# Batch 1's q loads placed between the gate/value and the out-projection weights, with new emission orders for every chunk

## Chip, cores, metric

One core of one Trainium2 chip. The metric is the device time of one execution in microseconds; a kernel's figure is the median of its runs. Profile times count from the start of the profiled span, which is about 2 us shorter than the device time.

## The reference, cut to what matters

```python
# 8 batches x 8 heads, 576 positions, head dim 64
q_s = softmax over the last dim of q;  k_s = softmax over the sequence of k
kv  = einsum('bhsd,bhse->bhde', k_s, v)
att = einsum('bhsd,bhde->bhse', q_s, kv)          # -> x: 4608 tokens x 512
out = (silu(x @ w_gate) * (x @ w_val)) @ w_out    # 512 -> 1536 -> 512
```

The attention is small. The feed-forward block is nearly all of TensorE's work and consumes `x` in chunks of 512 tokens.

## The kernel before

Engines run programs fixed at build time. The author writes the order as strings of tokens ("plans"), one plan for each kind of chunk; each token emits instructions on one or more engines, and each engine executes its own instructions in the order of emission. The tokens:

- `a`..`g`, `v`, `G`, `U`, `I`, `J`: first feed-forward product. `A`..`F`, `H`, `O`, `S`: out-projection; `E` and `H` also emit four stores each.
- `eq`, `ek`, `ns`, `cv`: exponentials, row sums and v cast of a coming batch. `nm0`, `nm1`: GpSimd product that normalizes q, and the DMA transpose of its result, for head groups 0 and 1.
- `load`: six loads (q, k, v for two head groups) of the batch after that. `kv`: the k-v matmuls. `xx`: the attention output, the first reader of the transposed q.

```python
def load(b, G, what, src, after=None):
    raw[what, b, G] = ld.tile([128, 2, T * 64], FP32, tag=what, ..., bufs=2 if what == "v" else 3)
    d = nc.sync.dma_start(out=raw[what, b, G], in_=ap)
    if after is not None:
        tc.add_manual_dep(d.ins, after.ins.name, SYNC, reason="order of loads")
...
def tr_dma(b, G):
    qt = at.tile([128, T, 2, 64], BF16, tag="qtd", name="qtd")
    nc.sync.dma_start_transpose(out=qt..., in_=s["qs"]...)      # same queue as the loads
...
elif nm == "nm":
    norm_mul(b, G, nc.vector if alt else nc.gpsimd)
    tr_dma(b, G)
elif nm == "lo":
    ...
    load_group(b + 1, 0)
    load_group(b + 1, 1)
elif nm == "xx":
    x_pair(b, nc.scalar if alt else nc.vector)   # matmuls xa, xz: first half reads
                                                 # transpose 0, second half transpose 1
...
PLAN = """
S002 G4 S022 S102 a0 b0 G10 d0 c0 A v0 a1 S042 eq0 S122 S142 S302 B S342 f0 S242
b1 ek0 U4 S322 D S222 ek1 e0 eq1 cv0 S202 C* v1 cv1 g0 ns0 F E d1 H* a2 ns1 c1 f1
silu nm0 b2 c2 nm1 e1 g1 d2* v2 a3 U10 f2 e2 load kv b3 g2 c3 d3 G5 v3 e3* f3 xx*
X0 G11 U5 X1 U11 g3* X3 X2
"""
```

`PLAN_B` is the prologue, `PLAN_0` chunk 0, `PLAN` the steady chunks 1 to 5, `PLAN_N` and `PLAN_E` the rest.

The softmax here doesn't subtract the row's maximum and nothing guards it: scores larger than these inputs give would overflow.

## Time and profile before

| | before |
|---|---|
| median time | 303.1 us (3 runs, 302.94 to 306.04) |
| TensorE busy / idle | 289.9 / 10.9 us of 300.8 |
| TensorE waits over 0.5 us | 2.6, 1.1, 1.0, 0.7 us, all before 76 us |
| steady chunk, start to start | 30.3 us |

TensorE's idle time is the quantity to watch: where it works without pause, only its instruction count and its clock set the time, and the change leaves the count as it is. The clock is given as the share of full speed that was granted: 1.00 is full, 0.50 is half. The prediction shows the lines.

### The profile page before, as it was taken

The page shows a single profiled execution, that of the slowest core. Times are in us where ns is not written, and L with a number is a line of the kernel's source. Part 1 is how long each engine was busy: PE and PEld are TensorE (multiplying, and loading weights), DVE is VectorE, ACT ScalarE, POOL GpSimd, SP SyncE. Part 2 cuts the span into 40 slices and gives each one's busy share as a digit, 9 for nine tenths or more (in the row PEclk, how much of TensorE's full clock was granted, in tenths as well). Part 3 has the DMA queues.
Part 4 walks back from the last instruction along what each step waited for, and adds up shares of the span by engine and source line. Part 5 has one row for each costly group of instructions (what it writes and reads, how often), then busy time and mean ns, then how long its engine had stood idle before and what let it go on. Part 6 is the DMA issues. An engine that isn't in the chain of part 4 may idle for free.

```text
span 300.8 us, 6895 instructions
## 1 busy us (share of the span) xinstructions
PE 289.9 (96%) x2644; PEld 227.9 (76%) x2644; DVE 232.3 (77%) x497; ACT 210.8 (70%) x385; POOL 136.6 (45%) x108
## 2 busy tenths in 40 slices
PE   8999978999999999999999999999999999999993
PEld 6878744577688758875887588758886888888882
DVE  3943846778898887888788778878888898895981
ACT  5754367787698579957994899489948776667530
POOL 1840156468208900890089008910794465275500
PEclk9999997999999999999999999999999999999999
DMA  7999999999002992289229931992190000600066
GB/s 268 265 173 207 224 396 316 313 252 327 0 3 60 161 391 83 55 174 375 92 49 175 352 117 29 200 360 105 39 183 0 2 0 4 139 3 0 2 140 140
DMA packets 38863, 46.43 MB, mean 154 GB/s; under 512 B 16304, under 2 KB 21936, under 8 KB 38832
## 3 DMA queue, kind: packets, MB, share of 16 engines
q1 hardware_dynamic: 33024, 41.30, 47.9%
q0 software_dynamic: 5808, 4.72, 10.2%
q8 instruction: 20, 0.33, 0.4%
q14 instruction: 11, 0.09, 0.1%
HBM read 37.75 MB, written 9.44 MB: 157 GB/s over the span
## 4 chain that ended last, share of the span: by engine, by line
PE 79%; DMA 14%; POOL 2%; DVE 1%; ACT 1%; SPq 0%; issue 0%; ACTq 0%; POOLq 0%; DVEq 0%
PE sx L384 20%; PE ox L526 14%; PE sw L384 10%; PE ow L526 7%; PE g_ps L435 7%; PE u_ps L435 7%; DMA wo<-in_moe_w_out_dram 6%; PE sy L384 5%; PE oy L526 3%; DMA qtd<-qs 3%; PE o_ps L473 3%; PE kv L192 3%; DMA v<-in_v_dram 3%; DMA q<-in_q_dram 2%; POOL wg L104 1%; POOL wv L104 1%
## 5 line engine op out<-in xcount | busy, mean ns | idle before, releaser
L418 POOL TENSOR_TENSOR hr<-sg,s 128x512 bf16<-128x512 f32 (+1 forms) x29 | 37.9, 1307 | 75.9 <-DVE s L417 74.9
L384 PEld LDWEIGHTS <-gt 128*128 128x128 f16 x576 | 56.2, 98 | 10.5 <-issue 0.7
L426 POOL TENSOR_TENSOR hr<-sg,s 128x512 bf16<-128x512 f32 (+1 forms) x28 | 35.6, 1271 | 35.4 <-ACT sg L425 35.4
L384 PE MATMUL sx<-xs,gt 128*128 128x256 f16 (+1 forms) x288 | 42.7, 271 | 0.0
L116 ACT COPY s<-sx 128x512 f32<-128x512 f32 (+1 forms) x66 | 38.2, 579 | 5.0 <-PE sx L384 4.2
L526 PEld LDWEIGHTS <-hs 128*128 128x128 bf16 x384 | 37.6, 98 | 5.4
L417 DVE TENSOR_TENSOR s<-sw,s 128x512 f32<-128x512 f32 (+1 forms) x36 | 24.5, 682 | 17.7 <-PE sw L384 17.4
L425 ACT ACTIVATE sg<-sx 128x512 f32<-128x512 f32 (+1 forms) x36 | 21.2, 590 | 19.9 <-PE sx L384 14.7
L152 POOL TENSOR_TENSOR qs<-eq,rr 128x1152 bf16<-128x1152 bf16 x14 | 29.5, 2120 | 10.5 <-DVE rr L147 10.5
L384 PEld LDWEIGHTS <-wg 128*128 128x128 f16 x288 | 27.7, 98 | 5.2
L421 DVE TENSOR_TENSOR s<-sx,s 128x512 f32<-128x512 f32 (+1 forms) x36 | 24.5, 680 | 8.9 <-ACT s L116 4.7
L526 PEld LDWEIGHTS <-hr 128*128 128x128 bf16 x288 | 28.2, 98 | 3.3
L410 ACT ACTIVATE sg<-s 128x512 f32<-128x512 f32 (+1 forms) x36 | 22.5, 626 | 8.0 <-DVE s L408 7.9
L143 DVE TENSOR_REDUCE rs<-eq 128x18 f32<-128x1152 bf16 x16 | 21.5, 1343 | 8.5 <-ACT eq L127 8.5
L116 ACT COPY s<-sw 128x512 f32<-128x512 f32 (+1 forms) x34 | 19.8, 583 | 8.9 <-PE sw L384 3.8
L408 DVE TENSOR_TENSOR s<-sy,s 128x512 f32<-128x512 f32 (+1 forms) x36 | 24.3, 675 | 1.6 <-ACT s L116 1.1
L435 PE MATMUL g_ps<-xt,wg 128*128 128x512 f16 (+1 forms) x96 | 24.3, 375 | 0.0
L526 PE MATMUL ox<-wt,hs 128*128 128x256 f16 x192 | 23.6, 273 | 0.0
L435 PE MATMUL u_ps<-xt,wv 128*128 128x512 f16 (+1 forms) x96 | 23.4, 375 | 0.0
L384 PE MATMUL sy<-xt,wg 128*128 128x256 f16 (+1 forms) x144 | 21.4, 271 | 0.0
L384 PE MATMUL sx<-xt,gt 128*128 128x256 f16 (+1 forms) x144 | 21.4, 271 | 0.0
L384 PE MATMUL sw<-xs,wv 128*128 128x256 f16 (+1 forms) x144 | 21.4, 271 | 0.0
(99 smaller groups left out, 571.4 us busy)
## 6 DMA issues: line engine op xcount, KB each, us to landing
q<-in_q_dram SPq DMA_DIRECT2D x16, 576.0 KB, 6.0
k<-in_k_dram SPq DMA_DIRECT2D x16, 576.0 KB, 8.3
v<-in_v_dram SPq DMA_DIRECT2D x16, 576.0 KB, 8.4
out_dram<-o_sb SPq DMA_DIRECT2D x72, 128.0 KB, 2.4
wo<-in_moe_w_out_dram POOLq DMA_DIRECT2D x3, 512.0 KB, 18.3
wg<-in_moe_w_gate_dram POOLq DMA_DIRECT2D x2, 512.0 KB, 11.5
wv<-in_moe_w_val_dram POOLq DMA_DIRECT2D x2, 512.0 KB, 13.0
wg<-in_moe_w_gate_dram POOLq DMA_DIRECT2D x2, 256.0 KB, 5.5
```

Of the source, the lines that this page charges most:

```text
L116: nc.scalar.copy(out=out, in_=in_)
L143: nc.vector.reduce_sum(out=rs, in_=s["eq"].rearrange("p t h d -> p (t h) d"), axis=mybir.AxisListType.X)
L152: eng.tensor_mul(s["qs"].rearrange("p t (h d) -> p (t h) d", d=64), s["eq"].rearrange("p t h d -> p (t h) d"), s["rr"].to_broadcast([128, ...
L384: nc.tensor.matmul(out=bank[:, h * j:h * j + h], lhsT=wgt(kk, j), rhs=rhs[:, kk, 0:h], start=first and j == 0 and kk == 0, stop=kk == 1, s ...
L408: nc.vector.tensor_add(self.s1, self.y[:, 0:w], self.s1)
L410: nc.scalar.activation(out=self.sa[:, 0:w], in_=self.s1, func=AF.Silu)
L417: nc.vector.tensor_add(self.s2, self.w[:, 0:w], self.s2)
L418: meng.tensor_mul(self.out(0), self.halves(self.sa), self.halves(self.s2))
L421: nc.vector.tensor_add(self.s5, self.x[:, 0:w], self.s5)
L426: meng.tensor_mul(self.out(1), self.halves(sb), self.halves(self.s5))
L435: nc.tensor.matmul(out=ps[:, 0:self.n], lhsT=w[:, kk, 128 * self.m:128 * self.m + 128], rhs=xt[:, kk, self.r:self.r + self.n], start=(kk = ...
L526: nc.tensor.matmul(out=dst[p][:, 0:HN], lhsT=lhs(kk, p), rhs=rhs(kk), start=start and i == 0, stop=i == HM - 1, skip_group_check=True,)
```

## The change

The intent: batch 1's q loads wait on the last gate slice rather than on the first out-projection slice, so its exponentials can start earlier; the plans are then reordered to use that. The diff, all five plans cut:

```diff
         tc.add_manual_dep(w_dma[0].ins, dmas["v", 0, 0].ins.name, SYNC, reason="order of loads")
+        load(1, 0, "q", q, after=w_dma[-2])
+        load(1, 1, "q", q)
         for m0 in (0, 4, 8):
             w_dma.append(wo_slice(m0, 4))
+        tc.add_manual_dep(w_dma[-3].ins, w_dma[-4].ins.name, SYNC, reason="order of loads")
...
-        load(1, 0, "q", q, after=w_dma[-3])
-        load(1, 1, "q", q)
         for G in range(NG):
-            load(1, G, "k", k)
+            load(1, G, "k", k, after=w_dma[-3] if G == 0 else None)
             load(1, G, "v", v)
...
         PLAN_B = """   (all of it reordered; its end:)
-        ... O21 xz00 kk1:1 xz01* ns0:2 O22 nm0:2 ek0:2 xz10* O31 cv1:2 xz11 eq1:2 O32 ek1:2
+        ... Q2 xz10 cv0:2 eq1:2 O31 ns0:2 O32 ek1:2 cv1:2 nm0:2
         PLAN_0 = """
-        a0 b0 ns1 load v0 ... c1 Y3 nm1 W0 g0 ... xx* e3 ...
+        a0 b0 G4 Y0 Y2 Y1 c0 ns1 ... d1 load e0 nm1 c1 ... e3 W2 xx* f3 ...
         PLAN = """
-        ... silu nm0 b2 c2 nm1 e1 g1 d2* v2 a3 U10 f2 e2 load kv b3 ... f3 xx* ...
+        ... E ns1 nm0 ek1 b2 g1 load nm1 d2 c2 v2 H* f2 e2 kv silu a3 b3 ... f3 xx* ...
         (PLAN_N and PLAN_E: the same tokens in other orders)
```

More of the change, by code (lines that the diff above doesn't have):

```diff
@@ L744 @@
         PLAN_B = """
-        I0 J0 I1 I2 J1 J2 I3 J3 I4 I5 J4 J5 I6 I7 J6 I8 Q0* J7 J8 I9 I10 Q2* Q1* J9 eq0:1
-        Q3 J10 eq1:1 I11 ns0:1 ns1:1 J11 ek0:1 ek1:1 nd1:1 O01 nd0:1* cv0:1 O11 O02* tr00
-        cv1:1 O12 tr10 tr11 kk0:1 eq0:2 cv0:2 load:2 tr01 O21 xz00 kk1:1 xz01* ns0:2 O22
-        nm0:2 ek0:2 xz10* O31 cv1:2 xz11 eq1:2 O32 ek1:2
+        I0 I1 J0 I2 J1 J2 I3 J3 I4 I5 J4 I6 J5 J6 I7 I8 J7 J8 eq0:1 ns0:1 eq1:1 I9 ns1:1
+        Q0 I10 J9 I11 J10 J11 Q1* O01 O11 ek0:1 O02 Q3* nd0:1* nd1:1* cv0:1 tr00 tr10
+        cv1:1 O21 tr11 ek1:1 tr01 kk0:1 O12 xz00 load:2 kk1:1 xz01* eq0:2 O22 ek0:2 xz11
+        Q2 xz10 cv0:2 eq1:2 O31 ns0:2 O32 ek1:2 cv1:2 nm0:2
 """
         PLAN_0 = """
-        a0 b0 ns1 load v0 Y0 G4 a1 Y2 Y1* kv U4 c0 d0 G10 f0 b1 c1 Y3 nm1 W0 g0 d1 v1 a2
-        e0 f1 e1 b2 c2 g1 d2 W1 v2 U10 a3 f2 G5 b3 g2 v3 e2 c3 d3* xx* e3 U5 f3 W2 X0 X2
-        X1 G11 U11 g3* X3 W3
+        a0 b0 G4 Y0 Y2 Y1 c0 ns1 G10 d0* v0 a1 U4 f0 Y3 W0 G5 b1 g0 d1 load e0 nm1 c1 v1
+        a2 f1 kv g1 b2 d2 e1 c2 v2 a3 f2 b3 c3 e2 U10 g2 d3 v3 e3 W2 xx* f3 U5 X0 W1 G11
+        X1 X3* W3 U11 g3 X2
 """
         PLAN = """
-        S002 G4 S022 S102 a0 b0 G10 d0 c0 A v0 a1 S042 eq0 S122 S142 S302 B S342 f0 S242
-        b1 ek0 U4 S322 D S222 ek1 e0 eq1 cv0 S202 C* v1 cv1 g0 ns0 F E d1 H* a2 ns1 c1 f1
-        silu nm0 b2 c2 nm1 e1 g1 d2* v2 a3 U10 f2 e2 load kv b3 g2 c3 d3 G5 v3 e3* f3 xx*
-        X0 G11 U5 X1 U11 g3* X3 X2
+        a0 b0 c0 G4 d0 G10 v0 a1* f0 S222 b1 A c1 S202 g0 S002 d1 S042 S242 S022 v1 e0
+        S122 B eq0 U4 S322 S102 S142 a2 e1 C S342 D ns0 cv0 eq1 U10 cv1 S302 F f1 ek0 E
+        ns1 nm0 ek1 b2 g1 load nm1 d2 c2 v2 H* f2 e2 kv silu a3 b3 g2 c3 d3* G5 v3 e3* f3
+        xx* U5 G11 X0 X2 X1 g3* U11 X3
 """
         PLAN_N = """
-        a0 b0 c0 d0 A v0 T0* f0 S002 a1 b1 g0 d1 c1 S022 S102 S222 v1 e0 a2 S202 f1 e1 b2
-        S042 c2 g1 d2 v2 S122 B f2 a3 T1 b3 c3 S242 S142 g2 e2 d3 S322 D v3 a4 f3 T2 C g3
-        T3 d4 b4 e3 c4 v4 f4 S302 F a5 g4 b5 S342 d5 v5 e4 c5* f5 E X0 X1 e5* X3 X2* g5*
+        S022 a0 b0 c0 d0 A v0 S042 T0* f0 T1 S142 S222 a1 b1 S122 c1 g0 e0 d1 v1 B f1 a2
+        b2 c2 g1 d2 S002 T2 S102 v2 a3 e1 e2 f2 D T3 g2 b3 d3 c3 v3 a4 f3 S302 b4 C S322
+        g3 v4 S202 d4* e3 c4 f4 a5 e4 b5 g4 d5 c5 S242 v5 S342 F f5 X0* e5 X2 E X1 g5* X3*
         H*
@@ L767 @@
         PLAN_E = """
-        S202 S042 S022 S002 A S142 S122 S102 B C S322 S302 S342 D S222 S242 E F H*
+        S042 S022 S222 A S002 S142 S102 B C S122 D S322 S202 S242 S302 S342 F E H*
 """
```

## The prediction

> **What bounds the kernel now.** I read the page first (busy times, slices), then TensorE's waits, then the chain that ended last, then the timelines of TensorE and of the load queue. The page says that TensorE (PE) is the bound:
>
> ```profile
> PE 289.9 (96%) x2644; PEld 227.9 (76%) x2644; DVE 232.3 (77%) x497; ACT 210.8 (70%) x385; POOL 136.6 (45%) x108
> ...
> PEclk9999997999999999999999999999999999999999
> DMA  7999999999002992289229931992190000600066
> ```
>
> A busy PE is not a PE at its peak, so I checked the pace: twelve 256-column matmuls of `ox` take 1.31 us in the chain, 109 ns each, and hardly vary anywhere after 76 us. So PE works at one steady pace, and its time falls only if idle time or slow clock goes. Idle is 300.8 - 289.9 = 10.9 us, of which about 5.2 us lie after the last matmul (the final copy and store). TensorE's waits name nearly all the rest:
>
> ```profile
> PE o_ps L473 <- DVE hr L324: 2.6, 1, 2.6
> PE warm_ps L256 <- DVE zero L604: 1.1, 1, 1.1
> PE xa L273 <- DMA qtd<-qs: 1.0, 1, 1.0
> PE kv L192 <- POOL vb L118: 0.7, 1, 0.7
> ```
>
> All are before 76 us. The 2.6 us hole (43.4 to 46.0 us) is also the cause of the 7 in the clock row: in one-microsecond windows the granted clock was 0.54, 0.50, 0.50 and 0.75 from 47 to 51 us, a loss of 1.7 us. Its origin is in the chain of waits, beside the second DMA stretch that matters:
>
> ```profile
> 16.33 16.65 DMA wo<-in_moe_w_out_dram
> 33.00 6.77 DMA q<-in_q_dram
> ...
> 65.96 9.55 DMA qtd<-qs
> ```
>
> Batch 1's q load is held until the first out-projection slice lands at 33.0, and itself lands at 39.8; VectorE then stands in its row sums while PE needs the product queued behind them. The DMA row is full for the first 75 us.
>
> **What the Trainium skill says.** (1) "DMA: Bandwidth & Descriptors", section "Queues, rings and completion order": SP owns one ring per DMA engine, and each engine consumes descriptors in ring order. "DMA Transpose (X-bar)" on the same page adds that the plain transpose is issued from SP or ACT; here it shares SP's queue with the loads. The trace agrees: a `qtd` transpose issued behind two stores, or behind another transpose alone, lands in 3.2 to 5.4 us; the only one that follows six loads took 9.6 us and landed 1.1 us after the last of them (65.00 + 9.4 = 74.4 against 65.96 + 9.55 = 75.5). (2) "TensorE: Matmul & The Clock Gate", Part 1: an idle PE falls to half clock, and needs a busy window of about 3.4 us to return. The trace agrees in size: half clock from 47 to 50.75 us, though here 2.6 us of idleness was enough.
>
> **The change, part by part.**
>
> (a) The early q loads. They now wait for the last gate slice, which lands at 14.86 + 13.6 = 28.5 us, in place of 33.0. The last value slice (30.5 us before) is nearly all that shares the DMA with them, so I expect q at 33 to 34.5 us, not 39.8 and 41.2. Row sums then lie before PE's products, and the 2.6 us hole and its 1.7 us of slow clock should go. The weights pay: the first out-projection slice is issued only after the last value slice has landed, so it lands nearer 36 than 33 us. The out-projection starts at 39.5, so that is close, but should hold within 1 us. Up to the start of chunk 0's matmuls (58.2 us) I expect 4 to 5 us gained.
>
> (b) Chunk 0 gives it back. In both kernels the second transpose of batch 2 stands behind six loads of batch 3. The queue:
>
> ```profile
> 58.48 1.35 SPq L180 DMA_TRANSPOSE qtd<-qs  x1
> 59.93 1.86 SPq L462 DMA_DIRECT2D out_dram<-o_sb  x2
> 61.84 0.58 SPq L89 DMA_DIRECT2D q<-in_q_dram  x1
> ...
> 65.00 0.85 SPq L89 DMA_DIRECT2D v<-in_v_dram  x1
> 65.96 5.14 SPq L180 DMA_TRANSPOSE qtd<-qs  x1
> ```
>
> What lets these loads go is the first transpose, after the GpSimd product `nm0`, which the new order puts behind the cast of batch 2's second v. That v landed at 60.2 (52.83 + 7.4); the DMA is full, so I expect it 2 to 3 us earlier at best, plus 1.1 us of cast and 2.1 us of product: transpose at 60 to 61, loads from 62, second transpose landed at about 75 again. PE would arrive near 70, waits some 5 us in place of 1.0, and loses about 1.7 us of clock. Sum of (a) and (b): -5 + 4.5 + 1.7, about +1 us.
>
> (c) The steady chunks. This is the step that I weigh most. The new chunk plan moves `load` from after both transposes to between `nm0` and `nm1`. The compiled order of the changed kernel's load queue confirms it: four stores of E, transpose, six loads, transpose, four stores of H, in chunks 1 to 4 (chunk 5 has no loads left). Before, it was eight stores, two transposes, six loads:
>
> ```profile
> 124.72 5.30 SPq L462 DMA_DIRECT2D out_dram<-o_sb  x8
> 130.14 3.19 SPq L180 DMA_TRANSPOSE qtd<-qs  x2
> 133.39 0.60 SPq L89 DMA_DIRECT2D q<-in_q_dram  x1
> ...
> 136.20 0.94 SPq L89 DMA_DIRECT2D v<-in_v_dram  x1
> ```
>
> The same chunk on PE: E ends at 124.0, and the `qtd` is used at 136.3 and 136.6:
>
> ```profile
> 122.72 1.47 PE L526 MATMUL ow<-wo,hs 128*128 128x256 f16 x12
> ...
> 136.28 0.33 PE L273 MATMUL xa<-qtd,kn 64*64 64x320 bf16 x4
> ...
> 136.55 0.31 PE L273 MATMUL xa<-qtd,kn 64*64 64x320 bf16 x4
> ```
>
> Now the new chunk, counted from the end of E on PE. Store issue starts 0.7 us later (124.0 to 124.72); four stores at 5.30 / 8 = 0.66 us are 2.6 us; the first transpose's issue is 1.4 us; so the loads start at +4.7. From first load issue to last landing the steady chunks show 12.2 to 13.0 us (133.39 to 136.20 + 9.4; 163.99 to 167.01 + 10.0). Only one transpose is ahead now, not two, so up to a microsecond less: 12.1. The transpose lands 1.1 us behind, as in chunk 0: +17.9. PE in the new order has after E thirteen groups of 0.437 us, H of 1.31, `kv` of 1.15 and one G of 0.86: it is at the `xa` at +9.0. The wait is 17.9 - 9.0 = 8.9 us, in a kernel where nothing after it can make up PE time. After nearly 9 us idle the clock is half for a while; from the 1.7 us seen, and 2.6 us that the 64 first warm-up matmuls take beyond 109 ns each (9.6 - 7.0), I take 2.0. Four chunks times 10.9 is 43.6 us.
>
> (d) The remaining reordering (chunks 5 to 8, matmul groups, sums) keeps PE's instruction count; the order had no waits after 76 us, and I take 0, with perhaps half a microsecond in chunk 5. The tail stays.
>
> Sum: 303.1 + 1 + 43.6 = 347.7; I say 347.
>
> **The rivals.**
>
> Rival 1: the prologue gain is all that happens. The 2.6, 1.0, 0.7 and 1.7 us go, and the steady chunks hide the transposes: 297 to 300 us. For it: these plans look tuned, and the title names the landing times. Against it: the changed queue order is a fact of the build, and chunk 0 has already shown what a transpose behind loads costs. It needs the transpose to pass the loads.
>
> Rival 2: the transpose is only partly held, because transfers overlap in the queue or the loads run faster when nothing else moves. DMA moved 390 to 410 GB/s in the full microseconds of 138 to 144 us, so 3.54 MB need 9 us; with first bytes 1.5 us after issue the transpose lands at +16 and the wait is 7 us, with 1 us of clock: 303 + 4 x 8 = 335.
>
> Rival 3: the out-projection weights land too late, and PE waits at 39.5 us. From 2.4 us a slice (33.0 to 35.4 us for the second) I can see 1 to 3 us once; chunk 0's DMA bound would hide part of it. Worth at most 3 us.
>
> **Range and chances.** The mechanism of (c) rests on one measured case but needs no scheduling luck; only its size is soft: 7.8 to 9.5 us a chunk, 1 to 3 us of clock, times four, and 2 us either way in the prologue. That gives about 338 to 354; I widen the low side for rival 2. Range 330 to 356. Rival 1 keeps a few per cent of chance.
>
> **What would show it.** Right: TensorE's waits list `xa` (or its weight load) on DMA `qtd` five times, four of them of 8 to 10 us; the DMA part shows second transposes landing after about 10 us; the clock row dips after each; no `o_ps` wait of 2.6 us near 43 us; `eq` of batch 1 starts before 36 us. Wrong: steady transposes landing in 3 to 5 us although issued behind loads, or PE reaching the `xa` later than 9 us after E because it waits elsewhere (then the wait moves, and my sum counts it under the wrong name). A `o_ps` wait on `wo` would speak for rival 3.

## The result and the profile after

The changed kernel takes **355.92 us** (median of 4, 355.2 to 357.69) against 303.02 us. A ratio in this document is the mean time of one kernel's fast runs over that of the other's fast runs of the same rounds, so it is not quite the ratio of the medians; here it is 1.174 (95% interval 1.164 to 1.184).

The page of the changed kernel, its first part (busy time of engines) and its second (40 slices of the span):

```profile
PE 299.7 (85%) x2644; PEld 228.8 (65%) x2644; DVE 235.2 (66%) x485; ACT 211.4 (60%) x390; POOL 148.7 (42%) x115
...
PEclk9999999996999589995999769995899999999999
DMA  7999998690009900396006920099004500050055
```

The same 2644 matmuls keep TensorE busy for 9.8 us longer (299.7 - 289.9), and idle time grew from 10.9 to 54.0 us (353.7 - 299.7). The clock row has five dips, and each follows a stretch in which the DMA row is full. TensorE's waits name the cause (who waited, for whom, us in total, times, longest):

```profile
PE xa L273 <- DMA qtd<-qs: 39.9, 5, 8.8
PE o_ps L473 <- DMA wo<-in_moe_w_out_dram: 2.1, 2, 1.9
PE sx L384 <- ACT s L116: 1.4, 1, 1.4
```

One kind of wait, five times, holds 39.9 of the 54.0 us of idleness; it was 1.0 us before. The load queue of the changed kernel in chunk 1 (timeline: start, length of the issue, not of the transfer):

```profile
104.36 2.41 SPq L462 DMA_DIRECT2D out_dram<-o_sb  x4
106.88 1.32 SPq L180 DMA_TRANSPOSE qtd<-qs  x1
108.25 0.58 SPq L89 DMA_DIRECT2D q<-in_q_dram  x1
...
112.36 3.54 SPq L180 DMA_TRANSPOSE qtd<-qs  x1
```

and TensorE in the same chunk (timeline, with the wait and its releaser in brackets):

```profile
102.80 1.48 PE L526 MATMUL ow<-wo,hs 128*128 128x256 f16 x12 [0.21 <-DVE hs L502]
...
113.32 0.33 PE L273 MATMUL xa<-qtd,kn 64*64 64x320 bf16 x4
...
122.55 0.48 PE L273 MATMUL xa<-qtd,kn 64*64 64x320 bf16 x4 [8.79 <-DMA qtd<-qs]
```

The first half of `xa` goes through at 113.3 us; the second waits 8.79 us for the transpose that was issued behind six loads. The last of these, issued at 111.80, landed 9.6 us later, at 121.4; the transpose landed at 112.36 + 10.15 = 122.5. What follows runs at half clock. One-microsecond windows of the changed kernel (busy time of PE, PEld, DVE, ACT, POOL, then the granted clock, DMA share, GB/s):

```profile
123.00:124.00 1.00, 1.00 (x10) 0.28 (x3) 0.00 (x0) 0.92 (x3) 0.00 (x0) 0.50 0.11 39
...
126.00:127.00 1.00, 1.00 (x5) 0.47 (x4) 0.80 (x3) 0.13 (x1) 0.00 (x0) 0.51 0.00 0
127.00:128.00 1.00, 1.00 (x7) 0.58 (x6) 0.00 (x0) 1.00 (x2) 0.00 (x0) 1.00 0.00 0
```

From 122.55 to 127.0 the clock is 0.50, which loses half of 4.4 us, 2.2 us.

Where the 52.9 us of added span lie, from the start of each chunk's first `sy` group on TensorE in both timelines. In the kernel before, chunks 1 to 5 open with one `G4` group of 0.86 us ahead of that mark; the table counts it with its own chunk, so that both columns hold the same work:

| stretch | before | after | added |
|---|---|---|---|
| to chunk 0 | 58.55 | 57.02 | -1.5 |
| chunk 0 | 21.25 | 29.73 | +8.5 |
| chunks 1 to 4 | 30.29, 30.28, 30.28, 30.29 | 41.76, 41.24, 40.79, 41.15 | +43.8 |
| chunk 5 | 30.28 | 31.18 | +0.9 |
| the rest | 69.58 | 70.83 | +1.2 |

### The profile page after: what moved, and what is told of

Its sections match the earlier page's. It is cut to its first block, busy times and chain, and to the rows that moved or that the text cites. A ratio compares the mean times of both kernels' runs of the same rounds, so it can differ in the third digit from the quotient of the medians.

```text
span 353.7 us, 6939 instructions
## 1 busy us (share of the span) xinstructions
PE 299.7 (85%) x2644; PEld 228.8 (65%) x2644; DVE 235.2 (66%) x485; ACT 211.4 (60%) x390; POOL 148.7 (42%) x115
## 3 DMA queue, kind: packets, MB, share of 16 engines
q1 hardware_dynamic: 33024, 41.30, 40.3%
## 4 chain that ended last, share of the span: by engine, by line
PE 64%; DMA 25%; DVE 2%; POOL 2%; ACT 2%; issue 1%; SPq 1%; DVEq 0%; POOLq 0%; ACTq 0%
PE sx L384 16%; DMA qtd<-qs 14%; PE ox L526 11%; PE sw L384 7%; PE u_ps L435 7%; PE ow L526 6%; PE g_ps L435 5%; DMA wv<-in_moe_w_val_dram 4%; PE sy L384 4%; DMA wo<-in_moe_w_out_dram 4%; PE oy L526 3%; PE kv L192 2%; DMA v<-in_v_dram 2%; DVE hs L502 2%; DMA q<-in_q_dram 1%
## 5 line engine op out<-in xcount | busy, mean ns | idle before, releaser
L426 POOL TENSOR_TENSOR hr<-sg,s 128x512 bf16<-128x512 f32 (+1 forms) x29 | 37.1, 1278 | 132.1 <-ACT sg L425 132.0
L418 POOL TENSOR_TENSOR hr<-sg,s 128x512 bf16<-128x512 f32 (+1 forms) x31 | 41.1, 1327 | 13.6 <-DVE s L417 13.6
L116 ACT COPY s<-sx 128x512 f32<-128x512 f32 (+1 forms) x59 | 34.1, 579 | 15.4 <-PE sx L384 15.2
L450 DVE TENSOR_TENSOR hr<-sg,u_ps 128x512 bf16<-128x512 f32 (+1 forms) x24 | 16.2, 674 | 40.8 <-PE u_ps L435 40.2
L273 PE MATMUL xa<-qtd,kn 64*64 64x320 bf16 x48 | 4.6, 381 | 39.9 <-DMA qtd<-qs 39.9
L152 POOL TENSOR_TENSOR qs<-eq,rr 128x1152 bf16<-128x1152 bf16 x15 | 32.7, 2181 | 6.0 <-DVE rr L147 6.0
L116 ACT CAST xt<-xa 128x320 f16<-128x320 f32 (+2 forms) x28 | 9.2, 396 | 38.6 <-PE xa L273 38.6
L273 PEld LDWEIGHTS <-kn 64*64 64x64 bf16 x96 | 2.0, 118 | 42.6 <-DMA qtd<-qs 41.3
L435 PE MATMUL u_ps<-xt,wv 128*128 128x512 f16 (+1 forms) x96 | 29.2, 435 | 0.0
L435 PE MATMUL g_ps<-xt,wg 128*128 128x512 f16 (+1 forms) x96 | 28.3, 424 | 0.0
L447 ACT ACTIVATE sg<-g_ps 128x512 f32<-128x512 f32 (+1 forms) x24 | 14.2, 593 | 15.9 <-PE g_ps L435 15.9
```

Source lines behind the costliest of these rows:

```text
L116: nc.scalar.copy(out=out, in_=in_)
L152: eng.tensor_mul(s["qs"].rearrange("p t (h d) -> p (t h) d", d=64), s["eq"].rearrange("p t h d -> p (t h) d"), s["rr"].to_broadcast([128, ...
L418: meng.tensor_mul(self.out(0), self.halves(self.sa), self.halves(self.s2))
L426: meng.tensor_mul(self.out(1), self.halves(sb), self.halves(self.s5))
L435: nc.tensor.matmul(out=ps[:, 0:self.n], lhsT=w[:, kk, 128 * self.m:128 * self.m + 128], rhs=xt[:, kk, self.r:self.r + self.n], start=(kk = ...
```

## The experiments

The theory to test: a transpose that is in flight together with the loads lands only when the loads are done; TensorE waits for it and then runs at half clock. A ring is, as in the prediction, the list of work that one issuing engine has on one DMA engine. The rivals: the new order of everything else costs the time; or the second GpSimd product is late.

**1. The steady loads behind the second transpose.** One token of the changed kernel moves:

```diff
-        ns1 nm0 ek1 b2 g1 load nm1 d2 c2 v2 H* ...
+        ns1 nm0 ek1 b2 g1 nm1 load d2 c2 v2 H* ...
```

> The changed kernel with one token moved: in the steady chunk plan the six loads come right behind the second transpose's issue, not ahead of it; chunk 0 is left as it is. Theory (the transpose is held by the loads ahead of it in its ring): the four steady xa waits of 8.0 to 8.8 us and the 2.2 us of slow clock after each go, so 355.9 - 4 x 10.8 = about 313 us (309 to 316), steady second transposes land within 4 us of issue, and chunk 0's wait of 6.1 us stays. Rival (the new order of the other instructions costs the time, or the second GpSimd product is late): under 10 us gained, above 345 us.

Measured: 311.73 us, ratio 1.025 (1.020 to 1.031). This run's waits, and the summary of its `qtd` tile:

```profile
PE xa L273 <- DMA qtd<-qs: 6.4, 1, 6.4
```

```profile
DMA to landing us min/median/max: 3.2/3.2/10.5
```

The four steady waits are gone, chunk 0's is left, and the transposes land in 3.2 us, although the loads follow directly in the same queue. One token of the order makes 44 of the 53 us. Both rivals fall: the order of everything else stayed.

**2. The same in chunk 0.** As 1, and `load e0 nm1` in `PLAN_0` becomes `e0 nm1 load`.

> As e1_steady_load_last, and in chunk 0 too the loads are put behind the second transpose. Theory: chunk 0's wait of 6.1 us and its 3.0 us of slow clock go as well, so about 9 us less than e1_steady_load_last: 302 to 305 us, no xa wait over 1 us. If the prologue of the changed kernel were itself worth 4 to 5 us, as the prediction had it, 299 us. Rival: chunk 0 is bound by the DMA as a whole, so the wait moves to another consumer and under 4 us is gained over e1_steady_load_last.

Measured: 304.89 us, ratio 1.005 (1.000 to 1.009), 6.8 us below run 1. The five `xa` waits shrank to one of 0.3 us (the profile is of the slowest of the six executions). A wait of 2.7 us of `sx` for ScalarE took part of the place in chunk 0: ScalarE stands in the exponential of a q that lands late. So with all the transposes free, the early q loads and the new order gain nothing over the kernel before.

**3. The reverse: the kernel before with its steady loads moved forward.**

```diff
-        silu nm0 b2 c2 nm1 e1 g1 d2* v2 a3 U10 f2 e2 load kv b3 ...
+        silu nm0 load b2 c2 nm1 e1 g1 d2* v2 a3 U10 f2 e2 kv b3 ...
```

> The kernel before with one token of its steady plan moved: the six loads go between the first and the second product-and-transpose, nothing else of the change. Theory (transposes in flight with loads land only when these are done, PE waits and then runs at half clock): this alone makes most of the loss. The first transpose is issued at about +19.6 us of the chunk, the second lands some 14.5 us later, and PE needs it at +26 us: waits of about 8 us and 2.2 us of clock in four chunks, 303.9 + 4 x 10 = about 344 us (337 to 350). Rival (it takes the whole new order): under 320 us.

Measured: 347.54 us, ratio 1.148. TensorE's waits in this run:

```profile
PE xa L273 <- DMA qtd<-qs: 37.7, 4, 9.9
```

The position of one token is sufficient, with nothing else of the change in the kernel.

**4. The loads in another ring.** Program order as in the changed kernel; the steady loads are issued by ScalarE.

```diff
-                        load_group(b + 1, 0)
-                        load_group(b + 1, 1)
+                        eng = nc.scalar if ci > 0 else nc.sync
+                        load_group(b + 1, 0, eng)
+                        load_group(b + 1, 1, eng)
...   (load and load_group pass eng on)
```

> The changed kernel with its program order kept, but the steady chunks' six loads are issued from ScalarE's queue, so that they have another ring than the transposes, and the same 3.5 MB move at the same time. Theory (order within one ring): the second transpose shares with the loads but no longer stands behind them; it lands in 3 to 6 us in place of 9 to 10, the steady waits fall from 8.5 to 0 to 3 us, total 313 to 328 us (ScalarE pays some 3 us of issue a chunk). Rival (bandwidth: DMA engines full of loads, so any transfer is late): waits stay at 7 us or more, total above 345 us.

Measured: 349.08 us, ratio 1.150. The expectation missed: leaving the loads' ring did not free the transpose. In chunk 1 the two transposes were issued at 107.86 and 110.41 us and landed after 12.2 and 12.0 us. ScalarE had issued its last loads at 111.31 and 113.30, after both transposes, and they landed first: 113.30 + 6.6 = 119.9 against 120.1 and 122.4. Most of the time that TensorE lost was another wait: ScalarE's own instructions stood still for 6.8 us while it issued the loads, and TensorE waited for its copies (`sx` on ScalarE, 28.6 us in 5 waits, against 7.5 us for `qtd`). So this run says nothing on the time without the ring order, but it says that a transpose need not stand behind loads to be late. The DMA part of a 20 us window of this run, with one load group of six (q10, ScalarE's ring), two transposes and some stores (q1), tells why:

```profile
DMA packets 4641, 5.19 MB, mean 260 GB/s; under 512 B 2592, under 2 KB 2592, under 8 KB 4640
...
q10 hardware_dynamic: 1632, 3.54, 48.9%
q1 hardware_dynamic: 3008, 1.64, 40.9%
```

Each load has 272 packets (1,632 / 6). With the 33,024 that the changed kernel's page counts for 48 loads, 72 stores and 12 transposes, a store comes to 80 and a transpose to 1,184; eight stores and two transposes then make the 3,008 of q1. So one transpose moves its 0.29 MB in 1,184 small packets, and six loads their 3.54 MB in 1,632. The Trainium skill says in "DMA: Bandwidth & Descriptors", section "Queues, rings and completion order", that each DMA engine takes turns between rings packet by packet. The same view for 112 to 114 us shows it:

```profile
q10 hardware_dynamic: 304, 0.65, 83.9%
q1 hardware_dynamic: 294, 0.13, 23.2%
```

From 113 to 119 us the loads' ring moved 155 to 167 packets in each microsecond and the transposes' ring 158 to 171: packet against packet, so the transposes got 0.04 MB of a microsecond's 0.39. When the loads ran out, the transposes' ring moved 915 packets in the next microsecond (119 to 120). In the changed kernel, where all share one ring, it looks different: only 0 to 14 packets under 512 B moved in each microsecond from 110 to 119 us, then 492 and 676 in those from 119 and 121 us. There the second transpose came after the loads in the order of the ring. So the transpose is late in either ring, in two different ways.

**5. Work in place of the wait.** In the changed kernel, dummy matmuls between the two halves of `xa`:

```diff
             s = st.pop((b, G))
+            if G == 1 and 2 <= b < B - 1:
+                warm_up(45 if b == 2 else 65)
```

> The changed kernel with added work: between the two halves of the xa matmuls, where PE waits, 45 (chunk 0) or 65 (chunks 1 to 4) dummy matmuls of 256 columns, 4.9 and 7.1 us at full clock, a little shorter than the waits of 6.1 and 8.0 to 8.8 us. Theory (PE's idle time makes its clock fall to half, and this costs 3.0 us in chunk 0 and 2.2 us in each steady chunk beyond the wait): with more work the kernel gets faster by up to 3.0 + 4 x 2.2 = 12 us, 343 to 348 us, and the granted clock after the waits is 1.00. Rival (the slow stretch after the wait is not caused by the idleness): the same 356 us or more, clock still 0.5 after the waits.

Measured: 349.65 us, ratio 1.152: with 305 more matmuls the kernel is some 6 us faster than without them, but not the 8 to 13 us expected. The timeline of TensorE in chunk 1, then windows of the same chunk:

```profile
109.83 7.27 PE L256 MATMUL warm_ps<-zero 128*128 128x256 bf16 x65
119.48 0.33 PE L275 MATMUL xa<-qtd,kn 64*64 64x320 bf16 x4 [2.38 <-DMA qtd<-qs]
```

```profile
119.00:120.00 1.00, 0.52 (x9) 0.26 (x10) 0.00 (x0) 0.14 (x1) 0.00 (x0) 1.00 1.07 408
...
121.00:122.00 1.00, 1.00 (x3) 0.30 (x2) 1.00 (x3) 0.59 (x2) 0.00 (x0) 0.50 0.00 0
```

The dummies ended 2.4 to 2.5 us early in chunks 1 and 2, and the clock fell to 0.50 again. In chunk 0 only 1.0 us of idleness was left, the clock stayed at 1.00, and the chunk takes 26.4 us in place of 29.7. In the third and fourth steady chunks 1.2 and 1.5 us were left, the clock stayed at 1.00, and the periods are 39.3 and 39.5 us in place of 40.8 and 41.2. In chunks 1 and 2, where the clock fell all the same, the periods are no shorter (42.1 us each, against 41.8 and 41.2). So the half clock goes only where the idleness that is left is short, and with it goes its cost; it is the idleness that causes it.

**6. The q loads alone.** The kernel before with the three load edits of the diff, all plans as before.

> The kernel before with only the first part of the change: batch 1's q loads after the last gate slice, the out-projection slices after the last value slice, k after the first of these; all plans as before. Prediction's step (a): the 2.6 us o_ps wait on VectorE and its 1.7 us of slow clock go, 299 to 301 us. Reading of the changed kernel's trace: the out-projection slices land later (last at 44 to 45 us against 39.5 us), PE waits for them 1.7 to 2.1 us in place of the 2.6 us, and chunk 0 is bound by loads anyway: 302 to 304 us, the same within 0.5%.

Measured: 303.23 us, ratio 0.9997 (0.995 to 1.005). The 2.6 us `o_ps` wait on VectorE and the slow clock after it are gone from its profile, as the prediction's step (a) says. But 1.7 us of `o_ps` on the out-projection weights came in, 1.4 us of transposes on `qs`, and `kv` waits for a v cast rose to 3.1 us. The last is not the edit's alone: run 3, whose prologue is that of the kernel before, has a `kv` wait of 2.9 us in its trace. There the hole of 2.1 us cost no clock, and TensorE came to chunk 0 at 56.0 us, not 58.6. That `kv` starts at 61.6 us before, 61.2 in run 3 and 62.2 in run 6, however early chunk 0 begins. The loads only exchange one wait for others.

**7. Half of the loads ahead.** The changed kernel with three loads before the steady `nm1` and three behind.

```diff
-        ns1 nm0 ek1 b2 g1 load nm1 d2 c2 ...
+        ns1 nm0 ek1 b2 g1 lod0 nm1 lod1 d2 c2 ...
```

> The changed kernel with three of the six loads ahead of the steady second transpose and three behind it, chunk 0 unchanged. Theory (the wait is the time that the bytes ahead take, 1.77 MB at 395 GB/s or 4.5 us for three loads): steady waits of 8.0 to 8.8 us fall by 4.5 plus 1.5 us of earlier issue to 2 to 4.5 us, clock loss stays near 1.7 us where the wait is over 2.5 us; about 331 us (324 to 338). Rival (a fixed cost of any switch from load to transpose in the queue): waits stay above 7 us, above 348 us.

Measured: 340.78 us, ratio 1.125; outside the range of the theory, and far from its rival. The four steady waits are 3.65, 4.29, 4.44 and 3.54 us, within the 2 to 4.5 us expected; they fell by 3.5 to 5.1 us, 4.5 in the mean, which is what three loads were reckoned to take. I had counted an earlier issue on top of that, and the half clock stayed (0.50 over three windows of chunk 1, after 3.65 us of wait). The wait scales with the bytes ahead; it is not a fixed cost of the switch.

**8. No hold on the out-projection slices.** As run 2, without the dependency that the change adds.

```diff
-        tc.add_manual_dep(w_dma[-3].ins, w_dma[-4].ins.name, SYNC, reason="order of loads")
```

> As e2_both_loads_last, without the wait of the first out-projection slice for the last value slice (the dependency that the change adds). Reading: the slices follow the value weights without a pause and land near 40 us, so the o_ps wait of 1.7 us on out-projection weights goes; the q loads share with them and land later than 33 us, which the plan can bear up to about 35 us. 302 to 303.5 us, 1.5 us less than e2. Rival: the q loads land so late that VectorE or ScalarE blocks the products again, or the later wait of 2.7 us for ScalarE in chunk 0 grows by as much: no gain.

Measured: 306.20 us, ratio 1.010. A miss; the rival came. The `o_ps` wait is gone, but the q loads, which now share with these slices, land late, ScalarE stands in their exponential, and a new wait appears in its profile:

```profile
PE u_ps L310 <- ACT sg L321: 3.1, 1, 3.1
```

So the dependency that the change adds is right for its order.

**9. The loads on a third queue.** As run 4 with `nc.gpsimd` in place of `nc.scalar`; one look.

> The changed kernel with its steady loads issued from GpSimd, the third queue, so that ScalarE is not held as it was in e4_loads_other_ring. The six issues (about 0.75 us each) stand ahead of the second product, which comes some 4.5 us later. Theory formed after e4 (the DMA engines take packets in turn from the rings; a transpose has about 1,300 small packets, six loads about 1,540 of 2.3 KB, so a transpose in another ring is served packet against packet and lands only when the loads are nearly done): transposes that overlap with the loads land in 9 to 12 us, the waits stay at 4 to 8 us, 340 to 358 us. If only order within one ring mattered: landings of 3 to 5 us, waits under 2 us (the late product alone), 315 to 325 us.

Measured: 362.49 us in a single run (state unknown). In chunk 1 the first transpose, issued at 108.58 just before the loads, landed after 6.6 us; the second, issued at 115.52, 2.2 us after the end of the last load's issue, landed after 8.9 us, at 124.4; the last load had landed at 112.61 + 11.1 = 123.7. TensorE waited 8.8 us for it. Over the four chunks the landings lie between 5.4 and 17.9 us, so mostly outside the 9 to 12 us expected, and the time is above the 340 to 358 us; but again a ring of its own did not set the transpose free. ScalarE was not held this time, so run 4's confusion is not the cause. The run has a confusion of its own: the six issues took GpSimd 4.4 us, and the second product came that much later.

**10. The kernel before, chunk 0 mended.** The one place where the kernel before has its loads ahead of the second transpose:

```diff
-        a0 b0 ns1 load v0 Y0 ... c1 Y3 nm1 W0 g0 ...
+        a0 b0 ns1 v0 Y0 ... c1 Y3 nm1 load W0 g0 ...
```

> The kernel before with one token of chunk 0's plan moved: batch 3's six loads behind the second transpose of batch 2, as they stand in all of its other chunks. Theory: the transpose lands in under 5 us in place of 9.6, so the xa wait of 1.0 us in chunk 0 and the 0.7 us that ScalarE's copy loses go, 1.0 to 1.7 us faster than before of the same rounds. Rival (chunk 0 bound by the DMA as a whole): no gain.

Measured: 301.79 us, ratio 0.9956 (0.9917 to 0.9996), 1.3 us under the kernel before. The load queue of this run in chunk 0:

```profile
64.57 1.30 SPq L180 DMA_TRANSPOSE qtd<-qs  x1
65.92 0.58 SPq L89 DMA_DIRECT2D q<-in_q_dram  x1
```

No `xa` wait is left. It is the only version here whose interval lies below the kernel before, by less than half a percent; at the 2% bound it counts as the same.

**11. Two more moves on the changed order.** As run 8, and batch 2's second exponentials go behind the first copies of chunk 0, its first product ahead of the second v cast:

```diff
-        Q2 xz10 cv0:2 eq1:2 O31 ns0:2 O32 ek1:2 cv1:2 nm0:2
+        Q2 xz10 cv0:2 O31 ns0:2 O32 nm0:2 cv1:2
-        a0 b0 G4 Y0 Y2 Y1 c0 ns1 G10 ...
+        a0 b0 Y0 Y2 Y1 c0 eq1 ek1 G4 ns1 G10 ...
```

> As e8_no_wo_hold, with two more moves: batch 2's second pair of exponentials, which wait for q and k that land at 58 us, come after the first ScalarE copies of chunk 0 and not before them, and the first transposed product of batch 2 goes ahead of the second v cast on GpSimd. If the 2.7 us wait of sx on ScalarE and the half clock after it (1.9 us) are caused by ScalarE standing in that exponential, they go: 297.5 to 300.5 us, 1 to 2% under the kernel before. If the start of chunk 0 is bound by the landing of batch 2's second loads whichever order is used, the wait moves to kv or xa: 302 to 304 us.

Measured: 305.86 us, ratio 1.010; a miss, above the forecast and its rival. The `sx` wait on ScalarE that the moves aim at is gone, but run 8's 3.1 us `u_ps` wait is still there and here drops the clock.

**12. The same with the hold kept.**

> As e2_both_loads_last (out-projection slices held back as in the change), with the two moves of e12: batch 2's second exponentials after the first copies of chunk 0, its first product ahead of the second v cast. e12's trace showed the sx wait on ScalarE gone but 3.1 us of a new u_ps wait that comes from the q loads sharing with the out-projection slices; with the hold kept that wait should not appear. The o_ps wait of 1.7 us stays. e2's 304.9 us less 2.7 us of wait and 1.9 us of clock: 300 to 302 us. If the landing of batch 2's second v bounds chunk 0 in any order: 303 to 305 us.

Measured: 303.87 us, ratio 1.005 (1.002 to 1.008); outside the expected 300 to 302, and in the rival's 303 to 305, though not for the rival's reason. Its trace shows both effects at once: chunk 1 starts at 77.36 us, 2.4 us before the kernel before (79.80, its `G4` group counted with chunk 1), and the steady chunks then take 30.66 us each against 30.29. The new orders lose 3.5 us after that (301.9 - 77.36 = 224.5 against 300.8 - 79.80 = 221.0): 1.5 in the steady chunks, 0.9 in chunk 5 and 1.1 in the rest. So the gain is spent. Part of that are the five waits of 0.2 us of `ow` on VectorE; the rest I have not traced. This prologue with the old steady plans was not run.

## Why the prediction was right or wrong, point by point

**The bound.** Right. TensorE's instructions did not change; time came from its idleness and its clock alone.

**Step (c), the steady chunks.** Right in mechanism and, with some luck, in size. It had the loads' issue 4.7 us after the end of E, the transpose at +17.9 us, `xa` at +9.0 us and a wait of 8.9 us. Chunk 1 shows E's end at 104.1, the first load at 108.25 (+4.1), the landing at 122.5 (+18.4), and waits of 8.79, 8.55, 7.95 and 8.48 us. The half clock was put at 2.0 us a chunk and took 1.9 to 2.2. Four chunks were to cost 43.6 us and cost 43.8. That the sums meet so closely is luck: the waits are 33.8 us in all, not 35.6, and the new order itself costs 0.37 us a chunk (30.66 us in runs 1, 2 and 12, which have no steady transpose wait, against 30.29), which no step had counted. Runs 1 and 3 show that the one token is both needed and enough for this loss. The reason given, order within one ring, holds for this kernel: its small packets follow those of the loads, and in run 7 the waits scale with the loads ahead. What it left out is that another ring is no way out: runs 4 and 9 have transposes just as late in a ring that holds no loads. The statement that fits all runs is that the transpose must be ahead in the ring (run 1: 3.2 us) or the DMA engines must be free of loads.

**Step (a), the prologue.** The mechanism was right, the size was not. The q loads were issued at 28.6 us and landed at 32.6 and about 35, and the 2.6 us hole with its slow clock went. But the term for the weights was mis-sized: "nearer 36" for the first slice was 38.05 us, and the last landed at 45.5 us (33.10 + 12.40), so that out-projection waits of 2.1 us came in, beside smaller ones (0.5 us each on `qs` and on ScalarE). Chunk 0 started 1.5 us earlier, not 4 to 5, and not even that is clear of noise: single traces start it at 58.55, 56.02 and 58.06 us with the old prologue (before, runs 3 and 10) and at 57.02 and 56.1 to 58.7 us with the new one (after, runs 1, 2, 4, 5, 7 and 9). Run 6 has 57.16 without the new plans.

**Step (b), chunk 0.** The second transpose landed at 69.73 + 10.23 = 80.0 us, not 75: batch 2's second v came to the cast only at 60.7, and the first transpose left at 64.0 rather than 60 to 61. The wait was 6.1 us, TensorE then worked at half clock from 80 to 86 us, which took 3.0 us, not 1.7, and ScalarE's late exponential added 1.4 us. The sum of (a) and (b) was +1 us and is +7.0 (8.5 - 1.5). A slip in the sum, which counts 4.5 us for a wait of 5 in place of 1.0, changes little.

**Step (d).** Zero was taken; chunk 5 and the rest added 2.1 us (0.9 + 1.2). Run 12 shows that the new orders lose time there without any transpose wait; why was not traced.

**The rivals.** Rival 1 (the prologue gain is all) fell. Rival 2 (overlap softens the wait to 7 us) fell: the waits were 8 to 8.8 us. Rival 3 (weights too late) came true beside the main effect, with 2.1 us against the 1 to 3 us given. The total of 347 was low by what (a), (b) and (d) missed: +7.0 us in place of +1, and +2.1 in place of 0, make the 8 us. Two readings were slightly off: the half clock before ended at about 50.5 us, not 50.75 (the 0.75 is the mean of one window), and the terms of the range add up to about 337 to 356, not 338 to 354.

## What to carry to other kernels

When a short transfer that an engine will need soon shares DMA engines with large prefetches, issue the short one first, in the same queue, and read the queue's compiled order to be sure; another queue did not help here. A prefetch that is needed a whole chunk later should be emitted after every transfer of the current chunk. On a TensorE-bound kernel count an idle gap with the slow clock that follows it, and if the gap can't be closed, dummy matmuls pay only if they leave little of it.

## What the Trainium skill lacked or had wrong

- "TensorE: Matmul & The Clock Gate", Part 1 and the advice on gaps, speak of an idle window of about 3.4 us and of gaps over 3 us. Here 2.38 us (run 5) and 2.6 us (before) of waiting were enough for half clock, while 2.07 us (run 3) and 1.0 to 1.5 us (run 5) were not. The same 3.1 us wait kept full clock in run 8 and lost it in run 11, which agrees with the page's free-running window. So do the lengths: worked out from the one-microsecond windows, the half clock lasted 3.4 us (before, 47.1 to 50.5; run 5, chunk 1), 6.8 us (after, 79.2 to 86.0) and 10.2 us (after, 116.9 to 127.0), one, two and three times the page's 3.4. So what a gap of 2 to 3 us costs seems to be a matter of its phase.
- "DMA: Bandwidth & Descriptors", section "DMA Transpose (X-bar)", gives constraints but no time beside other traffic (a bandwidth stands elsewhere on the page). A 128x1152 bf16 transpose lands in 3.2 us alone, in 9.2 to 10.4 us behind six loads of 576 KB in its ring, and in 10.4 to 15.1 us beside them in another ring (run 4). That it moves as 1,184 packets of under 512 B for 0.29 MB, so that turns by packet favour the loads, is not said.
- The same page's section "Issuing engines are not separate DMA queues" says that several issuing engines save only issue time. Run 4 agrees and adds a price: six loads issued from ScalarE held its own instructions for 6.8 us in chunk 1 and up to 9.0 us in the others.
